# A chunked delta rule and a feed-forward layer on one Trainium2 core: the triangular inverse by 32x32 blocks and substitution in place of seven levels of doubling

## The chip, the cores and the metric

The kernel runs on one core of one Trainium2 chip, written in Python against a tile framework. The framework's scheduler sets the order of instructions on each engine, gives out the buffers of its pools and adds the semaphore waits. The engines are PE (TensorE), DVE (VectorE), ACT (ScalarE), POOL (GpSimd) and SP (which here only issues DMAs); each works through its own queue in order. The metric is the device time of one execution in microseconds (us).

## The reference

Two parts, in float32 (the inputs moe_w_in and moe_w_out arrive as float64):

```python
# q, k, v: (B=4, H=8, S=768, D=48); beta: (4, 8, 768)
k_n = k / (np.linalg.norm(k, axis=-1, keepdims=True) + 1e-06)
for t in range(S):
    y[:, :, t] = einsum('bhd,bhde->bhe', q[:, :, t], state)
    v_old = einsum('bhde,bhd->bhe', state, kt)
    state = state + bt * einsum('bhd,bhe->bhde', kt, vt - v_old)
x = y.transpose(0, 2, 1, 3).reshape(3072, 384)
h = x @ w_in                                  # w_in: 384 x 2048
out = (h * sigmoid(1.702 * h)) @ w_out        # w_out: 2048 x 384
```

The loop over time is done in chunks of 128 tokens. With T = I + strictly-lower(diag(beta) Kn Kn^T) for a chunk, it is U = T^-1 (beta V - beta Kn S), Y = Q S + strictly-lower(Q Kn^T) U, S += Kn^T U. T^-1 is a 128x128 triangular inverse for every chunk, batch and head: 6 x 4 x 8 = 192 of them.

## The kernel before

A unit is one chunk c of one batch b, all eight heads: 6 x 4 = 24 units, in the order c outer, b inner. Batches don't depend on each other; within a batch the state S_bd carries from chunk to chunk.

- load (L71) issues three DMAs on SP per unit (K, q into QP, V), two units ahead.
- prepare (L197) makes what doesn't need the state: normalised keys kn (POOL: L204 ksq, L208 rn by pow, L211; DVE: L206 sum, L209, L210), kb = beta kn (L212), beta V (L215), their transposes on PE (psT, L223: kn, kb, q, four each), the scores psG (L237, 256 columns, 48 rows of contraction) and their masked eviction LM (L241 DVE, L246 POOL).
- The rest of prepare (L252 to L294) is the inverse by doubling. X holds the inverses of T's diagonal blocks of size s; seven levels s = 1, 2, ..., 64. A level does psE = T X (L259), E = psE times a mask (L264, DVE), psXT (L280) and psX (L288), each evicted by ACT (L284, L293). Each line is four 128x128x128 matmuls for each of two halves hh of the heads.
- advance (L298) is the step of a unit: psK (L305), R = V - psK (L310), psU = XT R (L313), U (L317), psS (L322) and S_bd (L345), psY (L330, L335), x (L340, ACT), three transposes psXT (L351) into xT (L352).
- The feed-forward part of chunk c runs over the tokens of all four batches (512) and is handed out in four steps, one per unit of chunk c + 1 (L402): mm1 (L357) does four ph of three matmuls of 512 columns for each gT tile, each ph evicted by the gelu on ACT (L367); mm2 (L370) does sixteen matmuls of 384 columns for one po, copied by DVE (L378) and stored by SP (L379).
- load_weights (L176) and from_double (L134) bring the weights in 14 parts: a DMA on ACT's queue and fourteen DVE operations (L156 to L170) that make float32 of float64.

The order is that of the scheduler, which starts from the driver's order: while PE works at prepare(n + 1), advance(n) and a quarter of the feed-forward part of the chunk before are placed between. PSUM is split into ps_big (4 buffers: psT, psG, psE, psXT, psX), ps_seq (2: the step) and ps_moe (2: ph and po).

```python
    for n, (c, b) in enumerate(units):
        ...
        if n + 1 < len(units):
            prepare(n + 1)
        ...
        advance(n, xTs[c])
        if c > 0:
            feed_forward(c - 1, xTs[c - 1], b)
```

Of the kernel before, what the change touches and what calls it, by code (L numbers as in the profile page):

```python
# [9 lines left out]
I32 = mybir.dt.int32  # L10
I64 = mybir.dt.int64
# [7 lines left out]
def kernel(  # L19
# [28 lines left out]
    NTB = B * C  # L48
    FQ = 4
    assert S % C == 0 and H == 8 and D <= DP and DM == H * D == KC * 128  # L50
    assert NTB == 512 and B == 4 and FC == 4 * FQ
# [6 lines left out]
    ps_moe = ctx.enter_context(tc.tile_pool(name="ps_moe", bufs=2, space=PSUM))  # L58

    units = [(c, b) for c in range(NC) for b in range(B)]  # L60

    # rows of 64 to a head, so that a transposed head starts at partition 0 or 64
    KN = [cpool.tile([128, H, DP], F32, name=f"KN{i}") for i in range(3)]
    KB = [cpool.tile([128, H, DP], F32, name=f"KB{i}") for i in range(2)]
    QP = [cpool.tile([128, H, DP], F32, name=f"QP{i}") for i in range(3)]
    for t in KN + KB + QP:
        nc.vector.memset(t, 0.0)
# [3 lines left out]
    def load(n):  # L71
        c, b = units[n]
        K = io.tile([128, H, D], F32, tag="K", name="K", bufs=2)
        V = io.tile([128, H, D], F32, tag="V", name="V", bufs=4)
        for dst, src in ((K, k), (QP[n % len(QP)][:, :, 0:D], q), (V, v)):
            nc.sync.dma_start(
                out=dst, in_=src[b, :, c * C : (c + 1) * C, :].rearrange("h p d -> p h d")
            )
        loaded[n] = K, V

    bt = cpool.tile([NBH, S], F32, name="bt")
# [5 lines left out]
    ident = cpool.tile([128, 128], F32, name="ident")  # L87
    make_identity(nc, ident)
    upper = cpool.tile([128, 1, 128], F32, name="upper")
    nc.gpsimd.memset(upper, 1.0)  # L90
    nc.gpsimd.affine_select(
        out=upper, in_=upper, compare_op=ALU.is_ge, fill=0.0, base=-1,
        pattern=[[0, 1], [1, 128]], channel_multiplier=-1,
    )
    half = cpool.tile([128, H], F32, name="half")
    nc.gpsimd.memset(half, 0.5)

    def block_mask(name, s, transposed=False):
        """I - M: M is 1 in the lower left (upper right, transposed) quarter of each 2s block."""
        m = cpool.tile([128, 128], F32, name=name)  # L100
        nb = 128 // (2 * s)
        nc.gpsimd.memset(m, 0.0)
        part = m.rearrange("p (n j) -> p n j", j=2 * s)
        part = part[:, :, s : 2 * s] if transposed else part[:, :, 0:s]
        lo = 0 if transposed else s
        nc.gpsimd.memset(part, -1.0)
        nc.gpsimd.affine_select(
            out=part, in_=part, compare_op=ALU.is_ge, fill=0.0, base=-lo,
            pattern=[[-2 * s, nb], [0, s]], channel_multiplier=1,
        )  # L110
        nc.gpsimd.affine_select(
            out=part, in_=part, compare_op=ALU.is_ge, fill=0.0, base=lo + s - 1,
            pattern=[[2 * s, nb], [0, s]], channel_multiplier=-1,
        )
        make_identity(nc, m, nomemset=True)
        return m.rearrange("p (o j) -> p o j", o=1)

    levels = [1, 2, 4, 8, 16, 32, 64]
    emask = {s: block_mask(f"em{s}", s) for s in levels}
    emask_t = block_mask("em1t", 1, True)  # L120

    S_bd = cpool.tile([128, B, NP, 2, D], F32, name="S_bd")
    nc.vector.memset(S_bd, 0.0)
# [10 lines left out]
    def from_double(dst, src, n):  # L134
        """dst: n float32 to a partition; src: as many float64, rounded to nearest.

        DVE has no float64: the words are taken apart. The upper 23 bits of the fraction with
        the exponent moved (896 less, which in its low 8 bits flips the top one) make a float,
        the last 29 bits a second one of that scale, and their sum is rounded once. What
        float32 hasn't the exponents for becomes 0 or inf.  # L140
        """
        raw = wk.tile([128, n], I64, tag="gT", name="raw", bufs=4)
        nc.scalar.dma_start(out=raw.rearrange("p (f d) -> p f d", d=src.shape[-1]), in_=src)
        words = raw.bitcast(I32).rearrange("p (n two) -> p n two", two=2)
        lo, hi = words[:, :, 0], words[:, :, 1]
        tmp = wk.tile([128, 2, n], I32, tag="gT", name="tmp", bufs=4)
        t0, t1 = tmp[:, 0], tmp[:, 1]
        t0f, w = t0.bitcast(F32), dst.bitcast(I32)
        ts, stt, tt = (
            nc.vector.tensor_scalar, nc.vector.scalar_tensor_tensor, nc.vector.tensor_tensor,  # L150
        )
        AND, OR, XOR = ALU.bitwise_and, ALU.bitwise_or, ALU.bitwise_xor
        SHL, SHR = ALU.logical_shift_left, ALU.logical_shift_right
        SIGN, INF = -(1 << 31), 0x7F800000

        ts(w, hi, 0x0FFFFFFF, 3, op0=AND, op1=SHL)  # L156
        stt(out=w, in0=hi, scalar=SIGN, in1=w, op0=AND, op1=OR)
        stt(out=w, in0=lo, scalar=29, in1=w, op0=SHR, op1=OR)
        ts(w, w, 0x40000000, None, op0=XOR)
        ts(t0, w, SIGN | INF, None, op0=AND)  # L160
        ts(t1, lo, 0x1FFFFFFF, None, op0=AND)
        stt(out=t0f, in0=t1, scalar=2.0**-52, in1=t0f, op0=ALU.mult, op1=ALU.mult)
        tt(dst, dst, t0f, op=ALU.add)

        ts(t0, hi, 20, 0x7FF, op0=SHR, op1=AND)
        ts(t1, t0, 897.0, -1.0, op0=ALU.is_ge, op1=ALU.mult)
        stt(out=t1, in0=t0, scalar=1150.0, in1=t1, op0=ALU.is_le, op1=ALU.mult)
        stt(out=w, in0=t1, scalar=SIGN, in1=w, op0=OR, op1=AND)
        ts(t1, t0, 1150.0, float(INF), op0=ALU.is_gt, op1=ALU.mult)
        tt(w, w, t1, op=OR)  # L170

    N_IN, F_OUT = 1024, 2
    parts_in = KC * DFF // N_IN
    n_parts = parts_in + FC // F_OUT

    def load_weights(part):  # L176
        if part < parts_in:
            j, f0 = part % KC, part // KC * N_IN
            dst = w_in[:, j, f0 : f0 + N_IN]
            src = moe_w_in[j * 128 : (j + 1) * 128, f0 : f0 + N_IN].rearrange(  # L180
                "p (o f) -> p o f", o=1
            )
            n = N_IN
        else:
            f0 = (part - parts_in) * F_OUT
            dst = w_out[:, f0 : f0 + F_OUT, :].rearrange("p f d -> p (f d)")
            src = moe_w_out[f0 * 128 : (f0 + F_OUT) * 128, :].rearrange("(f p) d -> p f d", p=128)
            n = F_OUT * DM
        if src.dtype == F32:
            nc.scalar.dma_start(out=dst.rearrange("p (f d) -> p f d", d=src.shape[-1]), in_=src)  # L190
        else:
            from_double(dst, src, n)

# [1 line left out]
    ready = {}  # L195

    def prepare(n):  # L197
        c, b = units[n]
        K, V = loaded.pop(n)
        kn, kb, qp = KN[n % len(KN)], KB[n % len(KB)], QP[n % len(QP)]  # L200
# [11 lines left out]
        nc.gpsimd.tensor_tensor(  # L212
            kb[:, :, 0:D], kn[:, :, 0:D], bc.broadcast_to([128, H, D]), op=ALU.mult
        )
        nc.gpsimd.tensor_tensor(V, V, bc.broadcast_to([128, H, D]), op=ALU.mult)  # L215

        knT = wk.tile([128, NP, 128], F32, tag="knT", name="knT")
        kbqT = wk.tile([128, 2, NP, 128], F32, tag="kbqT", name="kbqT", bufs=3)
        for src, dst, on_act in ((kn, knT, 0), (kb, kbqT[:, 0], 1), (qp, kbqT[:, 1], 1)):
# [4 lines left out]
            if on_act:  # L224
                nc.scalar.activation(dst, psT, ACT.Copy)  # L225
            else:
                nc.vector.tensor_copy(dst, psT)  # L227

        # LM[hh][:, j, 0] = T^T, LM[hh][:, j, 1] = strict_upper(Kn Q^T), head 2j + hh
        LM = []  # L230
        for hh in range(2):
            lm = wk.tile([128, NP, 2, 128], F32, tag="LM", name="LM", bufs=4)
            pr = slice(hh * 64, hh * 64 + D)
            for g in range(NP // 2):
                psG = ps_big.tile([128, 2, 2, 128], F32, tag="big", name="psG")
                for i in range(2):
# [12 lines left out]
            )  # L249
            LM.append(lm)  # L250

        X, XT = [None, None], [None, None]  # L252
        for s in levels:
            last = s == levels[-1]
            E = [None, None]
# [180 lines left out]
```

## Time and profile before

| | before |
|---|---|
| median of 3 runs | 1660.29 us (1658.6 to 1660.74) |
| span of the profiled execution | 1659.9 us |
| PE busy | 1581.8 us, 95% of the span |
| DVE / ACT / POOL busy | 557.4 / 413.0 / 243.1 us |
| matmul records on PE | 10254 |
| DMA | 33.05 MB, 81526 packets, mean 20 GB/s |

The profile shows one execution. Its times are us from the span's start, and ns where a mean of one instruction is given. In a row of a timeline come start, length, engine, line, operation, the tile written and the tiles read, the shape and the count, and in square brackets how long the engine had been idle and who ended that. In a row of a group come the count, busy us and mean ns of one, then the idle time before them and its releasers. In a row of a window: the stretch, its length, busy time and count of each engine (PE, PEld, DVE, ACT, POOL), the granted PE clock (1.00 is full), the DMA share and GB/s. In the chain of waits a row is start, length and what the chain ran through; "issue" is time in which nothing that the profile shows was waited for. In an excerpt of the order stand the line, the operation, the tile written and those read, the shape of the result and a count.

### The profile page before, as it was taken

To read this page: it belongs to the slowest core of one execution; us is meant where nothing else is said; L and a number is where in the kernel's file an instruction comes from. 1 tells how busy PE (TensorE), PEld (TensorE's weight loads), DVE (VectorE), ACT (ScalarE), POOL (GpSimd) and SP (SyncE) were. 2 spreads that over 40 slices of the span, in tenths; PEclk is the share of its full clock that TensorE was granted. 3 is DMA by queue.
4 is the path that set the end of the run, shared out by engine and by line. 5 is a ranking of instruction groups with operands and counts; after the bars stand their busy time and mean duration, and the time that the engine had idled before them with its cause. 6 is when DMAs were issued, how large, how long until landed. Compare 5 with 4: busy or idle time off the path is not lost.

```text
span 1659.9 us, 23464 instructions
## 1 busy us (share of the span) xinstructions
PE 1581.8 (95%) x10254; PEld 1303.3 (79%) x10254; DVE 557.4 (34%) x866; ACT 413.0 (25%) x698; POOL 243.1 (15%) x265
## 2 busy tenths in 40 slices
PE   3887889999999999999999999999999999999999
PEld 3887789968779779688797797886978978869645
DVE  7998993322223212222222132222221321222000
ACT  0321223323213133232132331222322313323020
POOL 7224111220101101201111012011010110000000
PEclk9987989999999999999999999999999999999999
DMA  4211200000000000000000000000000000000000
GB/s 105 90 56 53 91 20 10 15 15 6 10 20 6 24 6 11 15 6 20 24 6 10 6 11 24 6 19 15 6 10 10 16 10 1 1 1 1 20 0 19
DMA packets 81526, 33.05 MB, mean 20 GB/s; under 512 B 75504, under 2 KB 78576, under 8 KB 80656
## 3 DMA queue, kind: packets, MB, share of 16 engines
q1 hardware_dynamic: 78336, 18.88, 5.3%
q10 hardware_dynamic: 3088, 12.68, 2.2%
q8 instruction: 80, 1.31, 0.3%
q14 instruction: 22, 0.18, 0.0%
HBM read 26.84 MB, written 4.72 MB: 19 GB/s over the span
## 4 chain that ended last, share of the span: by engine, by line
PE 50%; issue 33%; POOL 9%; DVE 5%; DMA 3%; POOLq 0%; ACT 0%; ACTq 0%
PE psE L259 15%; PE psXT L280 13%; PE psX L288 10%; PE po L373 6%; PE ph L363 3%; DMA K<-in_k_dram 3%; POOL rn L208 2%; POOL LM L246 2%; POOL V L215 2%; POOL KN L211 1%; PE psU L313 1%; DVE E L264 1%; POOL ksq L204 1%; PE psS L322 1%; DMA V<-in_v_dram 1%
## 5 line engine op out<-in xcount | busy, mean ns | idle before, releaser
L264 DVE TENSOR_TENSOR E<-psE,em 128x512 f32<-128x512 f32 x336 | 231.5, 691 | 493.6 <-PE psE L259 493.2
L280 PE MATMUL psXT<-XT,E 128*128 128x128 f32 x2304 | 310.2, 279 | 10.7 <-DVE E L264 10.5
L280 PEld LDWEIGHTS psXT<-XT,E 128*128 128x128 f32 x2304 | 279.2, 191 | 15.9 <-DVE E L264 14.3
L284 ACT ACTIVATE XT<-psXT 128x512 f32<-128x512 f32 x240 | 143.3, 597 | 542.0 <-PE psXT L280 542.0
L373 PE MATMUL po<-w_out,gT 128*128 128x384 f32 x768 | 254.3, 488 | 0.0
L288 PE MATMUL psX<-E,XT 128*128 128x128 f32 x1920 | 253.6, 275 | 0.0
L363 PE MATMUL ph<-xT,w_in 128*128 128x512 f32 x576 | 253.6, 594 | 0.0
L259 PE MATMUL psE<-X,LM 128*128 128x128 f32 x1920 | 246.9, 281 | 0.1
L259 PEld LDWEIGHTS psE<-X,LM 128*128 128x128 f32 x1920 | 232.6, 191 | 4.4 <-ACT X L293 0.3
L288 PEld LDWEIGHTS psX<-E,XT 128*128 128x128 f32 x1920 | 233.7, 192 | 0.0
L373 PEld LDWEIGHTS po<-w_out,gT 128*128 128x128 f32 x768 | 143.5, 190 | 93.7 <-issue 0.5
L363 PEld LDWEIGHTS ph<-xT,w_in 128*128 128x128 f32 x576 | 107.1, 190 | 123.2 <-issue 122.9
L293 ACT ACTIVATE X<-psX 128x512 f32<-128x512 f32 x240 | 143.3, 597 | 68.0 <-PE psX L288 68.0
L211 POOL TENSOR_TENSOR KN<-K,rn 128x384 f32<-128x384 f32 x24 | 23.9, 995 | 607.7 <-PE psS L322 580.3
L367 ACT ACTIVATE gT<-ph 128x512 f32<-128x512 f32 x96 | 57.3, 597 | 204.4 <-PE ph L363 204.4
L246 POOL TENSOR_SCALAR_AFFINE_SELECT LM<-LM 128x512 f32<-128x512 f32 x48 | 32.5, 677 | 452.4 <-DVE LM L241 452.4
L259 PE MATMUL psE<-ident,LM 128*128 128x128 f32 x384 | 65.0, 322 | 35.4 <-POOL LM L246 35.4
L259 PEld LDWEIGHTS psE<-ident,LM 128*128 128x128 f32 x384 | 55.3, 222 | 47.8 <-POOL LM L246 47.8
L378 DVE COPY o<-po 128x384 f32<-128x384 f32 x24 | 13.4, 558 | 236.3 <-PE po L373 236.3
L237 PE MATMUL psG<-kbqT,knT 48*128 48x256 f32 x384 | 76.5, 411 | 3.2 <-DVE knT L227 2.5
L227 DVE COPY knT<-psT 128x512 f32<-128x512 f32 x24 | 16.5, 688 | 169.5 <-PE psT L223 169.5
L225 ACT ACTIVATE kbqT<-psT 128x512 f32<-128x512 f32 x48 | 26.2, 595 | 184.3 <-PE psT L223 184.3
(88 smaller groups left out, 1136.2 us busy)
## 6 DMA issues: line engine op xcount, KB each, us to landing
raw<-in_moe_w_in_dram ACTq DMA_DIRECT2D x6, 1024.0 KB, 5.7
raw<-in_moe_w_out_dram ACTq DMA_DIRECT2D x8, 768.0 KB, 4.4
K<-in_k_dram SPq DMA_DIRECT2D x24, 192.0 KB, 2.6
V<-in_v_dram SPq DMA_DIRECT2D x24, 192.0 KB, 2.8
QP<-in_q_dram SPq DMA_DIRECT2D x24, 192.0 KB, 2.7
out_dram<-o SPq DMA_DIRECT2D x24, 192.0 KB, 1.9
bt<-in_beta_dram ACTq DMA_DIRECT2D x1, 96.0 KB, 2.8
```

Of the source, the lines that this page charges most:

```text
L211: nc.gpsimd.tensor_tensor(kn[:, :, 0:D], K, rn.broadcast_to([128, H, D]), op=ALU.mult)
L237: nc.tensor.matmul(psG[:, i], lhsT=knT[pr, 2 * g + i, :], rhs=kbqT[pr, :, 2 * g + i, :], start=True, stop=True,)
L246: nc.gpsimd.affine_select(out=lm[:, :, 0, :], in_=lm[:, :, 0, :], compare_op=ALU.not_equal, fill=1.0, base=0, pattern=[[0, NP], [-1, 128]] ...
L259: nc.tensor.matmul(psE[:, j, :], lhsT=LM[hh][:, j, 0, :], rhs=ident if s == 1 else X[hh][:, j, :], start=True, stop=True,)
L264: nc.vector.tensor_tensor(E[hh], psE, emask[s].broadcast_to([128, NP, 128]), op=ALU.mult)
L280: nc.tensor.matmul(psXT[:, j, :], lhsT=E[hh][:, j, :], rhs=XT[hh][:, j, :], start=True, stop=True,)
L284: nc.scalar.activation(newT, psXT, ACT.Copy)
L288: nc.tensor.matmul(psX[:, j, :], lhsT=XT[hh][:, j, :], rhs=E[hh][:, j, :], start=True, stop=True,)
L293: nc.scalar.activation(X[hh], psX, ACT.Copy)
L363: nc.tensor.matmul(ph, lhsT=w_in[:, j, f * 128 : (f + 1) * 128], rhs=xT[:, j, :], start=(j == 0), stop=(j == KC - 1),)
L367: nc.scalar.activation(g[:, i, :], ph, ACT.Gelu_apprx_sigmoid)
L373: nc.tensor.matmul(po, lhsT=gT[c, f // FQ][:, f % FQ, b * C : (b + 1) * C], rhs=w_out[:, f, :], start=(f == 0), stop=(f == FC - 1),)
```

## The change

- The inverse is taken apart in 32x32 diagonal blocks. prepare leaves the scores of kn with kn scaled by beta in their rows (Nn, scaled as DVE evicts psG), and those with q in M (ACT, masked by POOL afterwards). kb is gone; V gets its beta in advance, on DVE. psG's heads alternate between the two halves.
- For each unit, four DMAs write the 32x32 diagonal blocks of Nn to DRAM (Nd) and one reads them back into NT, where every partition holds one block: 4 batches x 4 blocks x 8 heads = 128.
- invert(c) works on the 128 blocks of a whole chunk at once, on DVE: 15 substitution steps (a multiply and a sum each) on both 16x16 halves, then the 16x16 corner by two sets of four products (a multiply and a sum each); between them ACT copies one half of YB into X1 (L267 of the new kernel). YB goes to DRAM in four pieces Yb.
- assemble(n) reads a unit's blocks back (four DMAs into XT, four into XO), makes the 32x32 corners of the 64x64 blocks with ps1 and ps2 (PE), the 64x64 corner with ps3 and ps4, with 32x32 transposes on DVE, and evictions on DVE (P1, P3) and ACT (l32, L335, L359).
- The driver prepares and inverts a chunk as a whole: four assemblies and steps of chunk c, then prepare and invert of chunk c + 1, then the feed-forward part of chunk c, in two halves of two batches (256 columns for ph, two ph to a PSUM tile and a gelu).
- The weights come in 28 parts, with seven DVE operations each in place of fourteen, all asked for after the first chunk's steps. The DVE products P share the buffers of gT (five in place of four).

The diff, cut to its core:

```diff
 def prepare(n):
-    nc.gpsimd.tensor_tensor(kb[:, :, 0:D], kn[:, :, 0:D], bc.broadcast_to([128, H, D]), op=ALU.mult)
-    nc.gpsimd.tensor_tensor(V, V, bc.broadcast_to([128, H, D]), op=ALU.mult)
...
-    X, XT = [None, None], [None, None]
-    for s in levels:
...
+    for g in range(0, NP, 2):
+        ps = [ps_big.tile([128, 2, 2, 128], F32, tag="big", name="psG") for _ in range(2)]
+        for i in range(2):
+            for hh in range(2):
+                pr = slice(hh * 64, hh * 64 + D)
+                nc.tensor.matmul(ps[hh][:, i], lhsT=kqT[pr, g + i, 0, :], rhs=kqT[pr, g + i, :, :], start=True, stop=True)
+        for hh in range(2):
+            nc.vector.tensor_tensor(Nn[:, hh, g : g + 2, :], ps[hh][:, :, 0, :],
+                bhg[:, hh, g : g + 2].broadcast_to([128, 2, 128]), op=ALU.mult)
+            nc.scalar.activation(M[:, hh, g : g + 2, :], ps[hh][:, :, 1, :], ACT.Copy)
...
+    for blk in range(NB):
+        r = slice(blk * BS, (blk + 1) * BS)
+        nc.sync.dma_start(out=Nd[blk * H : (blk + 1) * H].rearrange("h i k -> i h k"),
+            in_=Nn[r, :, :, r].rearrange("i hh g k -> i (hh g) k"))
+    nc.sync.dma_start(out=NT[c][b * NB * H : (b + 1) * NB * H], in_=Nd)
+
+def invert(c):
...
+    for i in range(1, HS):
+        P = wk.tile([128, 2, i, i], F32, tag="gT", name="P", bufs=5)
+        tt(P, diag(Nf, i * BS, [[0, i], [1, i]]), diag(Yf, 0, [[BS, i], [1, i]]), op=ALU.mult)
+        red(diag(Yf, i, [[BS, i]]), P, axis=AX.X, op=ALU.add, negate=True)
+    X1 = wk.tile([128, HS, HS], F32, tag="X1", name="X1", bufs=1)
+    nc.scalar.activation(X1, halves(YB)[1].rearrange("p l i -> p i l"), ACT.Copy)
+    for j in range(0, HS, Q):
+        dots(A[:, j : j + Q, :], ..., Q, HS, HS - j, False)
+    for i in range(0, HS, Q):
+        dots(YB[:, 0:HS, HS + i : HS + i + Q], ..., HS, Q, i + Q, True)
+    for b in range(B):
+        nc.sync.dma_start(out=Yb, in_=YB[b * NB * H : (b + 1) * NB * H])
+
+def assemble(n):
+    for blk in range(NB):
+        nc.sync.dma_start(out=xt[r, :, :, r]..., in_=Yb[blk * H : (blk + 1) * H]...)
+    for p, hh in quads:
+        nc.sync.dma_start(out=XO[qd * BS : (qd + 1) * BS], in_=Yb[p0 : p0 + NP]...)
+    for p, hh in quads:
+        nc.scalar.activation(l32[o, :, o], Nn[od, hh, :, ev], ACT.Copy)
+        nc.vector.transpose(xe[o, :, o], xt[ev, hh, :, ev])
+    for g in range(NP):
+        nc.tensor.matmul(ps1[:, g], lhsT=l32[:, g, :], rhs=XO[:, g, :], start=True, stop=True)
+    nc.vector.tensor_copy(P1, ps1)
+    for g in range(NP):
+        nc.tensor.matmul(ps2[:, g], lhsT=xe[:, g, :], rhs=P1[:, g, :], start=True, stop=True)
+    for p, hh in quads:
+        nc.scalar.activation(xt[ev, hh, :, od], ps2[qd * BS : (qd + 1) * BS], ACT.Copy, scale=-1.0)
+    nc.vector.transpose(xa[e, :, e], flat[e, :, e])
+    nc.vector.transpose(xa[o, :, o], flat[o, :, o])
+    nc.vector.transpose(xa[o, :, e], flat[e, :, o])
+    for h in range(H):
+        nc.tensor.matmul(ps3[:, h, :], lhsT=Nf[hi, h, lo], rhs=flat[hi, h, hi], start=True, stop=True)
+    nc.vector.tensor_copy(P3, ps3)
+    for h in range(H):
+        nc.tensor.matmul(ps4[:, h, :], lhsT=xa[:, h, :], rhs=P3[:, h, :], start=True, stop=True)
+    nc.scalar.activation(flat[lo, :, hi], ps4, ACT.Copy, scale=-1.0)

 def advance(n, xT):
+    nc.vector.tensor_tensor(V, V, psK, op=ALU.subtract)
+    nc.vector.tensor_tensor(V, V, betaT[:, c, b].broadcast_to([128, H, D]), op=ALU.mult)
...
+def feed_forward(c, b0, xT):
+    for part in range(FC // FQ):
+        for i in range(0, FQ, 2):
+            ph = ps_moe.tile([128, 2, NTH], F32, tag="moe", name="ph")
+            ...
+            nc.scalar.activation(g[:, i : i + 2, :], ph, ACT.Gelu_apprx_sigmoid)
+    for i in range(HB):
+        po = ps_moe.tile([128, DM], F32, tag="moe", name="po")
...
+prepare_chunk(0)
+for c in range(NC):
+    for b in range(B):
+        assemble(c * B + b)
+        advance(c * B + b, xTs[-1])
+    if c == 0:
+        for part in range(n_parts):
+            load_weights(part)
+    if c + 1 < NC:
+        prepare_chunk(c + 1)
+    for i in range(B // HB):
+        feed_forward(c, i * HB, xTs[i])
```

More of the change, by code (lines that the diff above doesn't have):

```diff
@@ L79, in load @@
         loaded[n] = K, V
+    for t in KN + QP:
+        nc.vector.memset(t, 0.0)
     bt = cpool.tile([NBH, S], F32, name="bt")
@@ L195 @@
     ready = {}
+    NT = {}
+    Yd = {}
     def prepare(n):
@@ L223, in prepare @@
                 nc.tensor.transpose(psT[:, j, :], flat[:, j * 128 : (j + 1) * 128], ident)
[L224 to L236, printed above, removed]
+            nc.scalar.activation(kqT[:, :, i, :], psT, ACT.Copy)
@@ L237, in prepare @@
+        Nn = wk.tile([128, 2, NP, 128], F32, tag="Nn", name="Nn", bufs=4)
+        M = wk.tile([128, 2, NP, 128], F32, tag="M", name="M", bufs=4)
+        bhg = bc.rearrange("p (g hh) -> p hh g", hh=2)
+        for g in range(0, NP, 2):
[3 more added lines that the diff above has]
+                    pr = slice(hh * 64, hh * 64 + D)
                     nc.tensor.matmul(
-                        psG[:, i], lhsT=knT[pr, 2 * g + i, :], rhs=kbqT[pr, :, 2 * g + i, :],
+                        ps[hh][:, i], lhsT=kqT[pr, g + i, 0, :], rhs=kqT[pr, g + i, :, :],
@@ L298, in advance @@
     def advance(n, xT):
         c, b = units[n]
-        kn, V, kbqT, LM, XT = ready.pop(n)
-        R = V
+        kn, V, kqT, Nn, M = ready.pop(n)
+        xt = XT[n % len(XT)]
         if c > 0:
@@ L330, in advance @@
                 nc.tensor.matmul(
-                    psY[:, 2 * j : 2 * j + 2, :], lhsT=kbqT[:, 1, j, :], rhs=S_bd[:, b, j],
+                    psY[:, 2 * j : 2 * j + 2, :], lhsT=kqT[:, j, 1, :], rhs=S_bd[:, b, j],
                     start=(j == 0), stop=True, skip_group_check=True,
@@ new lines, in feed_forward @@
+    def feed_forward(c, b0, xT):
+        gT = []
+        for part in range(FC // FQ):
+            g = wk.tile([128, FQ, NTH], F32, tag="gT", name="gT", bufs=5)
+            for i in range(0, FQ, 2):
+                ph = ps_moe.tile([128, 2, NTH], F32, tag="moe", name="ph")
+                for u in range(2):
+                    f = part * FQ + i + u
+                    for j in range(KC):
+                        nc.tensor.matmul(
+                            ph[:, u], lhsT=w_in[:, j, f * 128 : (f + 1) * 128], rhs=xT[:, j, :],
+                            start=(j == 0), stop=(j == KC - 1),
+                        )
+                nc.scalar.activation(g[:, i : i + 2, :], ph, ACT.Gelu_apprx_sigmoid)
+            gT.append(g)
+        for i in range(HB):
+            b = b0 + i
+            po = ps_moe.tile([128, DM], F32, tag="moe", name="po")
+            for f in range(FC):
@@ L363, in mm1 @@
                 nc.tensor.matmul(
-                    ph, lhsT=w_in[:, j, f * 128 : (f + 1) * 128], rhs=xT[:, j, :],
-                    start=(j == 0), stop=(j == KC - 1),
-                )
-            nc.scalar.activation(g[:, i, :], ph, ACT.Gelu_apprx_sigmoid)
-        gT[c, part] = g
-    def mm2(c, b):
-        po = ps_moe.tile([128, DM], F32, tag="moe", name="po")
-        for f in range(FC):
-            nc.tensor.matmul(
-                po, lhsT=gT[c, f // FQ][:, f % FQ, b * C : (b + 1) * C], rhs=w_out[:, f, :],
-                start=(f == 0), stop=(f == FC - 1),
-            )
-        o = wk.tile([128, DM], F32, tag="o", name="o")
-        nc.vector.tensor_copy(o, po)
-        nc.sync.dma_start(out=out[b * S + c * C : b * S + (c + 1) * C, :], in_=o)
@@ L404, with prepare_chunk @@
-    for step in range(4):
-        feed_forward(NC - 1, xTs[NC - 1], step)
+                    po, lhsT=gT[f // FQ][:, f % FQ, i * C : (i + 1) * C], rhs=w_out[:, f, :],
+                    start=(f == 0), stop=(f == FC - 1),
+                )
+            o = wk.tile([128, DM], F32, tag="o", name="o")
+            nc.vector.tensor_copy(o, po)
+            nc.sync.dma_start(out=out[b * S + c * C : b * S + (c + 1) * C, :], in_=o)
+    def prepare_chunk(c):
+        for b in range(B):
+            n = c * B + b
+            prepare(n)
+            if n + 2 < len(units):
+                load(n + 2)
+        invert(c)
```

319 lines of the change are left out of this document (153 added, 166 removed).

## Prediction

> **What bounds the kernel now.** I read the page first (busy shares, chain by engine), then the chain of waits in order of time, then the timeline of one unit, then the groups by form. From the page and the chain:
>
> ```profile
> PE 1581.8 (95%) x10254; PEld 1303.3 (79%) x10254; DVE 557.4 (34%) x866; ACT 413.0 (25%) x698; POOL 243.1 (15%) x265
> PE 50%; issue 33%; POOL 9%; DVE 5%; DMA 3%; POOLq 0%; ACT 0%; ACTq 0%
> 1030.03 3.10 PE psE L259 x24
> 1096.01 3.10 PE psE L259 x24
> 1574.06 41.20 PE ph L363 x96
> 1615.25 41.30 PE po L373 x128
> ```
>
> TensorE is busy for 95% of the 1659.9 us. In the chain the same piece comes back after 65.98 us: that is one unit, and there are 24. The feed-forward part of the last chunk, alone on PE, is 41.2 + 41.3 = 82.5 us. In a unit's timeline the doubling stands in one stretch, from its second psE to its last psXT:
>
> ```profile
> 1031.02 2.10 PE L259 MATMUL psE<-E,LM 128*128 128x128 f32 x16
> ...
> 1060.50 2.10 PE L280 MATMUL psXT<-XT,E 128*128 128x128 f32 x16
> ```
>
> Those six levels last from 1031.02 to about 1062.4, 31.4 us; the first level adds 2. So 33 of a unit's 66 us are the inverse, and PE hardly pauses in it: the amount of matmuls is the bound.
>
> **What goes.** 24 x 33 = 800 us. If nothing came back, 860 us would be left. What comes back decides.
>
> **What comes in, on PE.** Prices of small matmuls, from the chain near the end (start, us, what):
>
> ```profile
> 1547.64 0.86 PE psK L305 x8
> ...
> 1549.82 1.72 PE psU L313 x16
> 1551.54 0.93 PE psY L330 x8
> ...
> 1553.15 1.72 PE psY L335 x16
> ...
> 1555.58 0.41 PE psXT L351 x3
> ```
>
> Two records make a float32 matmul, and a record costs 0.11 us at 48 and at 96 columns alike. The assembly of a unit has four ps1 and four ps2 of 32 columns (0.87 us per four) and eight ps3 and eight ps4 of 64 x 64, which no row shows: I take psY's 1.72 for each eight, the nearest row. The Trainium skill ("TensorE: Matmul & The Clock Gate", LDWEIGHTS) says that loading weights takes time by their columns; 64 columns would halve ps3 and ps4, and the total would be some 41 us lower. No row here has such a load, so I stay with the row.
>
> On PE the assembly of unit n+1 is now woven into the step of unit n (ps1 to ps4: assembly; psU, psS, psY, psXT2: the step):
>
> ```order
> L356 MATMUL ps4_2695<-P3_2693,XA0_87 64x64 x8
> L325 MATMUL ps1_2768<-XO_2751,L320_85 128x32 x4
> L377 MATMUL psU_2712<-V_1314,XT0_82 128x48 x8
> L330 MATMUL ps2_2775<-P1_2773,XE0_86 128x32 x4
> L386 MATMUL psS_2723<-U_2721,KN4_79 128x96 x4
> L394 MATMUL psY_2728<-S_bd_125,kqT_2090 128x96 x4
> L399 MATMUL psY_2728<-U_2721,M_2104 128x48 x8
> L349 MATMUL ps3_2787<-XT1_83,Nn_2159 64x64 x5
> L415 MATMUL psXT2_2745<-ident_108,x_2741 128x128 x3
> ```
>
> Before, a feed-forward matmul stood behind psU at this place:
>
> ```order
> L313 MATMUL psU_2865<-R_2863,XF_2447 128x48
> L363 MATMUL ph_2904<-xT_883,w_in_186 128x512
> L322 MATMUL psS_2876<-U_2874,KN2_75 128x96 x4
> L330 MATMUL psY_2881<-S_bd_175,kbqT_2155 128x96 x4
> L335 MATMUL psY_2881<-U_2874,LM_2174 128x48
> ```
>
> So the cover of the evictions changes: it was the feed-forward part, now it is the neighbour's assembly. The hops and evictions, in the timeline and the groups:
>
> ```profile
> 1062.44 0.54 PE L313 MATMUL psU<-R,XF 128*128 128x48 f32 x4
> 1062.82 1.52 PE L373 MATMUL po<-w_out,gT 128*128 128x384 f32 x4
> 1063.02 0.56 DVE L317 COPY U<-psU 128x384 f32<-128x384 f32 x1 [1.63 <-PE psU L313]
> 1067.89 0.49 ACT L340 ACTIVATE x<-psY 128x384 f32<-128x384 f32 x1 [4.65 <-PE psY L335]
> 1068.43 0.55 PE L351 MATMUL psXT<-ident,x 128*128 128x128 f32 x3
> L284 ACT ACTIVATE XT<-psXT 128x512 f32<-128x512 f32 x240 | 143.3, 597 | 542.0 <-PE psXT L280 542.0
> L264 DVE TENSOR_TENSOR E<-psE,em 128x512 f32<-128x512 f32 x336 | 231.5, 691 | 493.6 <-PE psE L259 493.2
> ```
>
> From PE's next matmul (1062.82) to the eviction 0.2 us; from x's end (1068.38) back to PE 0.05. ACT takes 0.49 at 384 and 0.60 at 512 elements, so 0.28 at 128; DVE 0.56 and 0.69, so 0.30. A woven unit: psU 1.72 + ps2 0.87 + psS 0.87 + psY 0.93 + 1.72 + ps3 1.72 + psXT 0.41 + psK 0.86 + ps4 1.72 + ps1 0.87 = 11.7 us, and 0.4 of waits (for x and P3): 12.1. The first unit of a chunk has no neighbour: its ps1 to ps4 (5.2) wait 0.55 for P1, 1.35 for four L335 copies, 0.94 for P3: 8.0. The last one's step alone is 6.9. **Stage A** (four assemblies and steps) = 8.0 + 3 x 12.1 + 6.9 = 51 us. DVE's seven 32x32 transposes a unit have no row; at a copy's 0.30 (128 elements) and 0.43 (256) DVE has under 6 us a unit beside PE's 12, so they are free; at four times that they would not be.
>
> **Stage B** (four prepares). With 256 columns a record:
>
> ```profile
> 1023.81 2.96 PE L237 MATMUL psG<-kbqT,knT 48*128 48x256 f32 x16
> ```
>
> 4 x 2.96 + 32 transposes at 0.11 (kb's sixteen are gone, with its POOL multiply, off the path) + 1.3 of waits for kqT = 17 us. The heads now alternate, which may overlap them; at the floor of 0.11 a record it would be 7 us. The 12 ph matmuls woven into A and B cost 5 us (24 of 192 half-width records, 41.2 in all). A 256-wide ph record is half a 512-wide one, 0.215, above the 0.11 floor: the halved feed-forward part costs nothing by itself.
>
> **The wait that comes in.** ACT behind a chunk's last evictions, before (gT is the gelu):
>
> ```order
> L284 ACTIVATE XF_4056<-psXT_4057 128x512
> L340 ACTIVATE x_4100<-psY_4087 128x384
> L367 ACTIVATE gT_4109<-ph_4110 128x512
> L367 ACTIVATE gT_4109<-ph_4115 128x512
> L367 ACTIVATE gT_4109<-ph_4120 128x512
> ```
>
> and now (M is the last eviction of prepare, X1 the copy inside the next chunk's inverse):
>
> ```order
> L214 ACTIVATE M_3147<-psG_3159 128x256
> L267 ACTIVATE X1_3225<-YB_88 128x256
> L432 ACTIVATE gT_3260<-ph_3261 128x512
> L432 ACTIVATE gT_3260<-ph_3269 128x512
> L432 ACTIVATE gT_3277<-ph_3278 128x512
> ```
>
> X1 waits for all 15 substitution steps of the next chunk, and the 16 gelus of this chunk stand behind it. ps_moe has two buffers, and the woven ph have filled both; PE's next ph waits. How long, from:
>
> ```profile
> L170 DVE TENSOR_TENSOR w_in<-w_in,tmp 128x1024 int32<-128x1024 int32 x6 | 7.3, 1218 | 0.0
> L206 DVE TENSOR_REDUCE ssq<-ksq 128x8 f32<-128x384 f32 x24 | 13.2, 551 | 2.1 <-POOL ksq L204 1.2
> 1071.96 0.17 DVE L209 TENSOR_SCALAR rn<-rn 128x8 f32<-128x8 f32 x1 [1.76 <-POOL rn L208]
> 1072.17 0.20 DVE L210 RECIPROCAL rn<-rn 128x8 f32<-128x8 f32 x1
> 1066.15 0.37 SPq L76 DMA_DIRECT2D K<-in_k_dram  x1
> K<-in_k_dram SPq DMA_DIRECT2D x24, 192.0 KB, 2.6
> out_dram<-o SPq DMA_DIRECT2D x24, 192.0 KB, 1.9
> ```
>
> The last Nn 0.6 (hop, 256 elements); four issues at 0.37 ahead of the last Nd 1.5; its landing 2.2 (between 1.9 and 2.6); NT's landing 2.1; 30 dependent DVE operations on 2 x 2480 elements, 1.04 ns each + 0.155 + 0.04 an operation = 11.0; X1 0.4; the first gelu 0.6; hops 0.2: **18.6 us** a chunk with PE idle. The rest of the inverse (16 operations on 10,240 elements, 14 us), Yd's round trip and the XT loads lie beside the feed-forward part, 77 us long, and cost nothing; without it some 20. Behind a stall the clock (last three columns: granted clock, DMA share, GB/s):
>
> ```profile
> 128.00:134.00 6.00, 4.96 (x44) 4.83 (x44) 6.00 (x8) 2.29 (x4) 0.00 (x0) 1.00 0.20 45
> 140.00:146.00 6.00, 6.00 (x27) 5.34 (x25) 6.00 (x10) 0.00 (x0) 6.00 (x1) 0.50 0.00 1
> 158.00:164.00 6.00, 6.00 (x50) 6.00 (x49) 5.39 (x11) 2.00 (x4) 0.00 (x0) 0.90 0.00 0
> 135.44 5.62 PE L237 MATMUL psG<-kbqT,knT 48*128 48x256 f32 x16 [2.49 <-DVE knT L227]
> ```
>
> It falls from 1.00 to 0.50 over idle gaps of a few us (psG takes 5.62 there instead of 2.96) and comes back after some 5 us of work: I charge 3 us. **A chunk**: 51 + 17 + 5 + 18.6 + (82.5 - 5.2) + 3 = 172 us (before 264), four times 688.
>
> **The start and the end.**
>
> ```profile
> L204 POOL TENSOR_TENSOR ksq<-K 128x384 f32<-128x384 f32 x24 | 20.1, 838 | 39.5 <-DMA K<-in_k_dram 39.5
> L208 POOL TENSOR_TENSOR rn<-ssq,half 128x8 f32<-128x8 f32 x24 | 42.3, 1763 | 58.5 <-DVE ssq L206 58.5
> L211 POOL TENSOR_TENSOR KN<-K,rn 128x384 f32<-128x384 f32 x24 | 23.9, 995 | 607.7 <-PE psS L322 580.3 <-PE psT L223 16.3 <-DVE rn L210 11.1
> L162 DVE SCALAR_TENSOR_TENSOR tmp<-tmp 128x1024 f32<-128x1024 int32 x6 | 7.3, 1217 | 0.0
> L162 DVE SCALAR_TENSOR_TENSOR tmp<-tmp 128x768 f32<-128x768 int32 x8 | 7.7, 958 | 0.1
> L159 DVE TENSOR_SCALAR w_in<-w_in 128x1024 int32<-128x1024 int32 x6 | 4.2, 697 | 0.0
> L159 DVE TENSOR_SCALAR w_out<-w_out 128x768 int32<-128x768 int32 x8 | 4.4, 556 | 0.0
> 1656.57 0.56 DVE L378 COPY o<-po 128x384 f32<-128x384 f32 x1 [9.76 <-PE po L373]
> ```
>
> POOL has 0.84 + 1.76 + 1.0 = 3.6 us a unit. On SP the first Nd stands behind a K load that waits for the fifth KN: I put that at 27 us and the last NT's landing at 43 (35 to 55), the inverse 25 behind it: 68. Then DVE: conversions 12 x (4 x 0.415 + 3 x 0.70) + 16 x (4 x 0.345 + 3 x 0.57) = 95, the first assemblies 21, the next prepares 11, gaps 10 (0 to 30): 205. The next inverse's steps stand behind all that on DVE, and X1 behind them: 217. The first feed-forward part ends at 217 + 77 + 2 = 296. The last chunk: 51 - 3.5 (no psS) + 82.5 + 1 = 131; from the last o to the span's end 3.4 us, as before.
>
> **Sum**: 296 + 688 + 131 + 3 = 1118 us. The span of the profiled execution, 1659.9, is 0.4 under the median of the runs, so nothing is corrected.
>
> **Rivals.** (1) *The gelu isn't held*, X1 being done before ph needs its buffer. Then 4 x 21.6 goes, and 29 at the start (po waits for the conversions to 205 instead): 1003 us. For it: only that the stall is read from two queues and no row; against: X1 needs the fourth unit's psG and four landings behind it. 8%. (2) *Slow clock all through A and B*: some 62 us of matmuls a chunk at half speed give 1118 + 4 x 62 + 45 = 1411; for half of the time 1265. For it: the 0.50 rows, after a gap of 2.49; against: PE pauses in A for 9% of the time, in pieces under 1.4 us. The Trainium skill ("TensorE: Matmul & The Clock Gate", Part 1) puts the fall after an idle window of about 3.4 us; by that rule only the gelu stall trips it and 1118 stands, and the 2.49 gap speaks for less than that. 12%. (3) *Slower than before*: the small transfers stand one behind another on SP. A unit has 14 (Nd, NT, Yb, XT, XO); all exposed at 2.6 they are 36 us, 24 times 874: some 1960. It decides from 23 us a unit, 9 of the 14; I count two a chunk. The Trainium skill ("DMA: Bandwidth & Descriptors", Specifications) says that pieces under 512 B are read, modified and written; these are 128 B, and K's of 192 B (48 floats a head) land in 2.6. 3%.
>
> **How the numbers follow.** The forecast has 77%. Its own unknowns: down 12 (ps3 and ps4 overlapped as psG is), 50 (psG at the floor), 20 (stall and start at their low ends), so 1035; up 72 (3 us more waiting a unit in A), 25 (start), so 1215, which takes in a part of rival 2. A change under 0.2%, 3 us, couldn't be told from none: 1%. Faster 96%, slower 3%.
>
> **What would show it.** Right: ACT idle for about 18 us a chunk before X1, PE as long before ph; the same piece coming back after 172 us; the clock at 1.00 in A. Wrong: ph running on behind psG, A taking 80, or PE waiting elsewhere for a landing of NT, XO or XT.

## The result and the profile after

| | before | after |
|---|---|---|
| median of the runs | 1660.51 us (1658.6 to 1662.05, 4 runs) | 1283.05 us (1276.61 to 1286.69, 4 runs) |
| ratio | | 0.772, 95% interval 0.770 to 0.774 |
| the profiled execution, span | 1659.9 us | 1281.6 us |
| mean granted clock | 0.98 | 0.77 |

The change is faster, by 377 us; 542 had been forecast (1118), and 1283 lies above the range of 1035 to 1215.

The page of after, with busy time, PE's and the clock's 40 slices, and the chain by engine:

```profile
PE 1024.0 (80%) x4974; PEld 837.8 (65%) x4974; DVE 438.9 (34%) x1020; ACT 203.5 (16%) x488; POOL 117.0 (9%) x112
PE   2408971199999299999389999479999669999998
PEclk9855665599758689857789857779956879955799
PE 31%; DVE 3%; DMA 1%; ACT 0%; SPq 0%; issue 0%; ACTq 0%
```

PE was busy for 95% before and is for 80% now, in a span 23% shorter, and the clock, which had been near 1.00, drops to about half in every chunk, also in slices where PE shows 9. Two losses are to be told apart. Both stand in the stretches of one chunk and of the end (columns: stretch, length, busy of PE, PEld, DVE, ACT and POOL, granted clock, DMA share, GB/s):

```profile
922.10:984.00 61.90, 59.81 (x316) 56.34 (x315) 18.23 (x45) 10.71 (x33) 4.05 (x4) 0.53 0.07 15
984.00:1013.60 29.60, 28.58 (x235) 24.18 (x233) 11.43 (x26) 11.34 (x29) 3.34 (x4) 1.00 0.19 36
1013.60:1038.00 24.40, 0.03 (x2) 0.00 (x0) 17.14 (x42) 2.38 (x7) 1.09 (x1) 0.59 0.07 16
1042.00:1117.60 75.60, 75.60 (x288) 54.58 (x287) 5.12 (x11) 8.36 (x14) 0.00 (x0) 1.00 0.10 22
1121.00:1199.00 78.00, 77.21 (x392) 72.65 (x393) 18.48 (x41) 10.84 (x30) 0.00 (x0) 0.50 0.02 4
```

The first row is most of stage A (assemblies and steps): PE is busy for 59.8 of 61.9 us, and the clock stands at 0.53. The second holds the rest of A, B and 16 of the 24 woven ph records at 1.00; the first eight of them, from 968.8 on, stand in the first row. The third is the pause, without PE work. The fourth is the feed-forward part. The last chunk's stage A (fifth row) runs at 0.50 throughout.

In the chain of the same chunk (start, length, what) the step's matmuls show what that costs:

```profile
922.29 0.82 PE ps L325 x8
923.48 1.09 PE ps L330 x8
...
931.60 3.44 PE psU L377 x16
...
952.18 3.44 PE psU L377 x16
...
974.68 3.28 PE psU L377 x16
...
991.38 1.86 PE psU L377 x16
```

psU takes 3.44 us where the prediction had 1.72, and a woven unit takes 20.6 us (931.60 to 952.18) where it had 12.1. Sixteen records come at 1.86 again once the clock is back, in the fourth unit. The pause, in the waits of PE and in ACT's timeline:

```profile
PE ph L428 <- ACT gT L432: 142.6, 5, 45.4
PE ps L325 <- DMA XO<-Yb: 42.1, 1, 42.1
```

```profile
1031.38 0.65 ACT L267 ACTIVATE X<-YB 128x256 f32<-128x256 f32 x1 [16.55 <-DVE YB L263]
1037.36 1.08 ACT L432 ACTIVATE gT<-ph 128x512 f32<-128x512 f32 x2 [5.33 <-DVE A L243]
```

PE waits 142.6 us for a gelu, five times, once 45.4. The gelu stands behind X1, as forecast, but after X1 it waits another 5.33 us for a reduction of the inverse (A, L243), with whose result it has nothing to do.

### The profile page after: what moved, and what is told of

It is laid out like the page before. It is cut to its first block, busy times and chain, and to the rows that moved or that the text cites. A ratio compares the mean times of both kernels' runs of the same rounds, so it can differ in the third digit from the quotient of the medians.

```text
span 1281.6 us, 12617 instructions
## 1 busy us (share of the span) xinstructions
PE 1024.0 (80%) x4974; PEld 837.8 (65%) x4974; DVE 438.9 (34%) x1020; ACT 203.5 (16%) x488; POOL 117.0 (9%) x112
## 5 line engine op out<-in xcount | busy, mean ns | idle before, releaser
L428 PE MATMUL ph<-xT,w_in 128*128 128x256 f32 x1152 | 284.6, 406 | 142.6 <-ACT gT L432 142.6
L428 PEld LDWEIGHTS ph<-xT,w_in 128*128 128x128 f32 x1152 | 230.9, 205 | 178.5 <-ACT gT L432 144.9
L377 PEld LDWEIGHTS psU<-V,XT 128*128 128x128 f32 x384 | 77.2, 304 | 1.6
L377 PE MATMUL psU<-V,XT 128*128 128x48 f32 x384 | 78.0, 383 | 0.0
L205 PE MATMUL psG<-kqT 48*128 48x256 f32 x384 | 62.9, 458 | 10.2 <-ACT kqT L194 8.0
L399 PE MATMUL psY<-U,M 128*128 128x48 f32 x384 | 68.9, 352 | 0.0
L399 PEld LDWEIGHTS psY<-U,M 128*128 128x128 f32 x384 | 68.3, 274 | 0.2
L205 PEld LDWEIGHTS psG<-kqT 48*128 48x128 f32 x384 | 42.9, 221 | 23.1 <-ACT kqT L194 13.3
L349 PE MATMUL ps<-XT,Nn 64*64 64x64 f32 x384 | 45.1, 293 | 5.6 <-ACT XT L335 5.6
L356 PE MATMUL ps<-P,XA 64*64 64x64 f32 x384 | 43.6, 295 | 5.4 <-DVE P L353 5.4
L193 PE MATMUL psT<-ident,KN 128*128 128x128 f32 x96 | 18.5, 325 | 35.9 <-POOL KN L186 23.1
```

What stands on the lines that cost most here:

```text
L205: nc.tensor.matmul(ps[hh][:, i], lhsT=kqT[pr, g + i, 0, :], rhs=kqT[pr, g + i, :, :], start=True, stop=True,)
L349: nc.tensor.matmul(ps3[:, h, :], lhsT=Nf[hi, h, lo], rhs=flat[hi, h, hi], start=True, stop=True)
L356: nc.tensor.matmul(ps4[:, h, :], lhsT=xa[:, h, :], rhs=P3[:, h, :], start=True, stop=True)
L377: nc.tensor.matmul(psU[:, h, :], lhsT=xt[:, h % 2, h // 2, :], rhs=V[:, h, :], start=True, stop=True)
L399: nc.tensor.matmul(psY[:, h, :], lhsT=M[:, h % 2, h // 2, :], rhs=U[:, h, :], start=(c == 0 and h == 0), stop=True, skip_group_check=True,)
L428: nc.tensor.matmul(ph[:, u], lhsT=w_in[:, j, f * 128 : (f + 1) * 128], rhs=xT[:, j, :], start=(j == 0), stop=(j == KC - 1),)
```

## The experiments

Ten kernels. Nine are timed against the kernel before on their chip, and the times are medians; the one with TensorE alone ran once.

**What the gelu waits for.** The inverse's products P and the gelu's output gT share one tag with five buffers. Three kernels take the candidates apart.

X1 on DVE:

```diff
-        nc.scalar.activation(X1, halves(YB)[1].rearrange("p l i -> p i l"), ACT.Copy)
+        nc.vector.tensor_copy(X1, halves(YB)[1].rearrange("p l i -> p i l"))
```

> X1 is copied by DVE instead of ACT, nothing else. Theory A (the gelus are held by X1 ahead of them on ACT, as the prediction had it): with X1 off that queue the feed-forward part runs on behind psG, TensorE's pauses of some 25 us a chunk go, five of them: 1283 - 115 to 125 = about 1160. Theory B (the first gelu is held longer by its buffer: gT and the inverse's products P share one tag with five buffers, and the trace has the gelu wait 25.3 us in five for a reduction of the inverse that ends up to 5.3 us after X1): the pause stays as long as it is, 1283 within 5.

Measured 1284.66 (ratio to before 0.773, interval 0.772 to 0.775): no change, theory B's number. PE's wait for the gelu is still there:

```profile
PE ph L428 <- ACT gT L432: 144.0, 5, 45.6
```

P with a buffer of its own:

```diff
-            P = wk.tile([...], F32, tag="gT", name="P", bufs=5)
+            P = wk.tile([...], F32, tag="P", name="P", bufs=1)
```

> P gets a tag and one buffer of its own, X1 stays on ACT. Theory A and B alike: the gelus now wait for X1 alone, which saves the 25.3 us that the trace shows behind X1 in five chunks: about 1258. If neither queue nor buffer holds them, nothing changes.

Measured 1143.9 (0.690, 0.685 to 0.695): 139 us faster, over five times what either theory gave it. The row of ph in the groups of this kernel (busy, mean ns, idle before):

```profile
L428 PE MATMUL ph<-xT,w_in 128*128 128x256 f32 x1152 | 279.2, 399 | 0.0
```

Its idle time is 0.0, with X1 still on ACT. ACT's order in one chunk says why:

```
after:                                   P with its own buffer:
L214 ACTIVATE M_3147<-psG_3159           L214 ACTIVATE M_2216<-psG_2228
L267 ACTIVATE X1_3225<-YB_88             L432 ACTIVATE gT_2346<-ph_2347
L432 ACTIVATE gT_3260<-ph_3261           ... (five more gelus)
L432 ACTIVATE gT_3260<-ph_3269           L267 ACTIVATE X1_2294<-YB_88
```

The scheduler had put the gelus behind X1 because a gT could have no buffer before the P's of the inverse were through. Without the shared buffer it puts six of them in front. X1's place on ACT was a symptom.

Both edits:

> Both edits: X1 on DVE and P with a buffer of its own. Theory B: only now is nothing of the inverse ahead of the gelus, TensorE's idle time before ph of 142.6 us goes but for the first chunk's wait for the weights (some 20 of its 45): about 1160, and the clock no longer falls between psG and ph. Theory A: the same as X1 alone.

Measured 1141.01 (0.689, 0.685 to 0.694): as P's buffer alone. The shared buffer is the whole pause; X1 is nothing.

**What holds the clock down in stage A.** Wide matmuls in the lead-in of a chunk, where PE waits for evictions:

```diff
+        if b == 0 and c > 0:
+            wide = ps_moe.tile([128, 512], F32, tag="moe", name="wide")
+            for i in range(3):
+                nc.tensor.matmul(wide, lhsT=P1..., rhs=w_in[:, 0, 0:512], start=True, stop=True)
```

and two each behind ps3 (from xt) and ps4 (from P3).

> Seven float32 matmuls of 512 columns with a result that nobody reads are added in the first unit of each chunk but the first: three behind ps2, two behind ps3, two behind ps4, where TensorE waits for evictions in the lead-in; 7 x 0.86 = 6 us of work a chunk, five chunks, some 15 of the 30 us in time that is idle now. Theory 1 (what the small matmuls do sets the clock, not the waits): the clock falls to 0.50 within one or two windows of 3.4 us behind the last wide one and stays there for the next two units as now: 1285 to 1305. Theory 2 (the waits of the lead-in drop the clock, and it then needs more than small matmuls to rise, but not to stay): the clock stays at 1.00 through the whole of stage A, which saves about half of the 58 us at 0.50 in four chunks and of the last chunk's 78: 1283 - 4 x 25 - 33 + 15 = about 1165.

Measured 1270.55 (0.764, 0.760 to 0.767), 12 us faster than after with some 30 us of matmuls more. Neither theory had that number. The windows of one chunk say how it comes about:

```profile
920.00:933.00 13.00, 13.00 (x90) 8.94 (x88) 3.52 (x9) 2.37 (x8) 1.03 (x2) 1.00 0.10 16
933.10:936.50 3.40, 3.19 (x30) 2.94 (x29) 1.95 (x8) 1.56 (x5) 1.33 (x1) 1.00 0.40 74
936.50:974.00 37.50, 37.50 (x193) 35.12 (x191) 11.36 (x26) 5.04 (x15) 0.83 (x1) 0.50 0.03 6
974.00:1005.00 31.00, 29.18 (x240) 24.75 (x239) 12.19 (x28) 12.03 (x30) 4.10 (x4) 1.00 0.19 35
```

The lead-in now runs at 1.00. Then comes a stretch of psY, ps2, psXT2 and the first records of psK and ps3, in which PE pauses for 0.2 of 3.4 us, and behind it the clock falls and stays at 0.50 through 37.5 us without a pause. So it falls late, as theory 1 has it: not for waiting. But what is bridged does hold, which theory 1 had not counted.

TensorE alone, with no wait at all:

```diff
+    for n in [512, 128, 96, 64, 48, 32, 48, 64, 96, 128, 256, 512, 48, 512]:
+        ps = ps_moe.tile([128, 512], F32, tag="moe", name=f"w{n}_")
+        for i in range(count):
+            nc.tensor.matmul(ps[:, 0:n], lhsT=wt[:, i % 8, :], rhs=mv[:, 0:n], start=True, stop=True)
```

> Nothing of the kernel is computed: the output is zeros. TensorE alone, float32 matmuls back to back with eight different weights of 128x128 loaded in turn, with no wait in them: 27 us at full clock each of 512, 128, 96, 64, 48, 32, 48, 64, 96, 128, 256, 512, 48 and 512 columns. Theory 1 (a window of 3.4 us counts by how much of it columns are streamed; in the traces the clock fell behind windows with under 0.38 to 0.41 of a full clock's columns and rose behind windows with over 0.8 of a half clock's): 128 columns hold 1.00; 96 (0.73 of the time at 0.11 us a record) hold it; 64 (0.48) is near the limit; 48 (0.36) and 32 (0.24) fall to 0.50 within two windows although TensorE never waits; on the way up 48 and 64 stay at 0.50, 96 is near the limit, 128 brings 1.00 back. A record of 48 columns takes 0.11 us at 1.00 and 0.22 at 0.50. Theory 2 (only time in which TensorE waits lowers the clock): 1.00 throughout behind the first stretch.

The chain, one row a stretch (512, 128, 96, 64, 48, 32 columns, then 48, 64, 96 and 128 again, and, after one of 256, a later stretch of 512):

```profile
18.87 28.50 PE w__100 L77 x62
47.38 27.24 PE w__133 L77 x244
74.62 27.22 PE w__257 L77 x244
101.84 27.22 PE w__381 L77 x244
129.06 46.63 PE w__505 L77 x244
175.69 52.03 PE w__629 L77 x244
227.72 52.08 PE w__753 L77 x244
279.80 52.08 PE w__877 L77 x244
331.88 29.41 PE w__1001 L77 x244
361.29 27.27 PE w__1125 L77 x244
...
415.33 26.61 PE w__1313 L77 x62
```

Two stretches of it with the same 64 columns, on the way down and on the way up:

```profile
104.00:128.00 24.00, 24.00 (x217) 24.00 (x217) 0.00 (x0) 0.00 (x0) 1.00 0.01 1
282.00:325.00 43.00, 43.00 (x203) 43.00 (x203) 0.00 (x0) 0.00 (x0) 0.50 0.00 0
```

PE is busy for the whole of both. On the way down 128, 96 and 64 columns hold 1.00 (27.2 us for 244 records, 0.11 each); at 48 the clock falls; on the way up 48 and 64 stay at 0.50 (52.1 us), and 96 brings 1.00 back. In columns: 62 records of 512 take 26.6 us at full clock (the last row), 1193 columns a us. At 0.11 us a record, 64 columns are then 48% of what could stream, 48 are 36%; at 0.50, 64 are 50% and 96 some 75% of what the half clock could stream. **A full clock stays at 48% and falls at 36%; a half clock stays at 50% and rises at 75%.** Theory 2 is out.

The kernels fit, by estimates from the counts and shapes of their rows: the woven unit from 931.60 to 952.18 streams 6784 columns, 330 a us, 55% of the half clock's, which lies between the 50% that left it down and the 75% that brought it up; the 3.4 us ahead of 936.50 above stream some 37% of a full clock's. Only the columns were varied, in one execution; whether weights on 64 rows, as those of ps3 and ps4, count like those on 128 was not tried.

The rule of the Trainium skill ("TensorE: Matmul & The Clock Gate", Part 1) that the clock falls after an idle window of about 3.4 us agrees in the length of the window (in these traces the clock changes at multiples of 3.413 us: its stretch at 0.50 in the last chunk of the kernel after is 78.51 us, 23 of them) and not in what counts as idle: PE was never idle here, and for 0.2 us in the 3.4 ahead of 936.50 above.

**The order of the program.** The second half of a chunk's feed-forward part is issued behind the next chunk's stage A:

```diff
+        if c > 0:
+            feed_forward(c - 1, HB, xT_held)
+        xT_held = xTs[1]
         if c + 1 < NC:
             prepare_chunk(c + 1)
-        for i in range(B // HB):
-            feed_forward(c, i * HB, xTs[i])
+        feed_forward(c, 0, xTs[0])
+        if c + 1 == NC:
+            feed_forward(c, HB, xT_held)
```

> Only the order of the program: the second half of a chunk's feed-forward part is issued behind the next chunk's stage A instead of ahead of it, with a third xT buffer; X1 and P as they are. TensorE then has wide matmuls between the small ones from the start of stage A. Theory 1 (what the matmuls do sets the clock): stage A stays at 1.00, its 58 us at 0.50 in each of four chunks cost about 25 less and the last chunk's 78 about 33 less; the pause of 25 us before ph stays: 1283 - 133 = about 1150. Rival (what holds the clock down in stage A is the chain of short waits behind each eviction, or the woven matmuls delay that chain as much as the clock gives): stage A grows by the 41 us it takes in, without a gain: 1270 to 1300.

Measured 1176.77 (0.707, 0.705 to 0.710): 106 us faster, 27 short of the sum. The windows of one chunk, stage A first, the pause third:

```profile
655.00:720.00 65.00, 64.52 (x441) 58.81 (x440) 23.47 (x59) 13.59 (x38) 10.12 (x10) 0.77 0.15 29
720.00:772.00 52.00, 51.36 (x260) 37.78 (x259) 8.39 (x22) 13.08 (x31) 6.31 (x6) 1.00 0.17 35
772.70:796.40 23.70, 0.89 (x9) 0.72 (x7) 17.79 (x43) 1.84 (x5) 1.09 (x1) 0.62 0.13 25
```

Stage A is at 0.77 instead of 0.53, and the pause is as long as it was.

The same order with P in its own buffer (and X1 on DVE, o and P1 with one buffer each):

> The same order, with P in a buffer of its own and X1 on DVE (o and P1 with one buffer each, for the space). If the shared buffer and the slow clock in stage A are two separate losses, their gains add up: 1141 less what the slow clock still costs there, 102 windows of 3.4 us at 0.50 = 348 us, half of them lost = 174, of which some 25 a chunk can come back: 985 to 1030. If one stands in for the other (the feed-forward part had covered the inverse, and half of it now lies in stage A): TensorE waits for XO instead, 20 us a chunk: 1080 to 1110.

Measured 996.1 (0.600, 0.598 to 0.602). One chunk, and the clock's slices of the page:

```profile
555.00:590.00 35.00, 34.32 (x305) 31.28 (x303) 18.04 (x46) 11.44 (x32) 6.50 (x6) 1.00 0.19 35
590.00:632.00 42.00, 41.73 (x242) 31.55 (x242) 8.46 (x21) 4.55 (x11) 6.58 (x6) 1.00 0.11 24
632.00:648.00 16.00, 15.36 (x110) 11.74 (x108) 5.29 (x14) 9.48 (x26) 3.27 (x3) 1.00 0.46 92
648.00:695.90 47.90, 47.90 (x195) 36.27 (x196) 28.28 (x59) 6.86 (x14) 1.09 (x1) 1.00 0.19 42
```

```profile
PEclk9999999999999999977999999999999999999999
```

A chunk takes 141 us, PE busy for 139 of it at 1.00. The two losses are separate, and the gains more than add up: 139 for the buffer and 106 for the order are 245, together they give 287. This version is the best of all that ran.

Some 30 of the 42 between 245 and 287 lie in stage A. With the order alone it falls as in the row above in three chunks (1 to 3), with both edits in one, the two sevens; 65 us at 0.77 lose some 15, an estimate from that row. Why the clock stays up in the other chunks was not looked into.

The first seven nines of that line are not a measurement. The trace's first record of the clock is at 185 us, and ahead of it the profile shows 1.00 whatever the clock is. The same sixteen records of psU show that it was at half:

```profile
140.24 3.63 PE L377 MATMUL psU<-V,XT 128*128 128x48 f32 x16
191.48 1.99 PE L377 MATMUL psU<-V,XT 128*128 128x48 f32 x16
```

**Two parts of the change alone, on the kernel before.** Each feed-forward matmul of 512 columns as two of 256:

> The kernel before, with each feed-forward matmul of 512 columns as two of 256, nothing else: the step of the prediction that priced the halves at nothing. By it, 1660 within 5. Rival (each record costs its weight load, or a fixed time, on top): 1152 more records at 0.1 us = 1660 + 115 = 1775.

Measured 1660.02 (0.999, 0.998 to 1.000): free, as priced. The new conversion of the weights:

> The kernel before with the new conversion of the weights, nothing else: 97 us of DVE in place of 176 in the first 260. TensorE pauses there for some 34 us between 40 and 280 and loses a few more by the clock. If DVE's share of that is what holds it: 1660 - 25 to 40. If the loads or the chain of each unit's evictions hold it: 1660 within 5.

Measured 1630.68 (0.980, 0.978 to 0.983): 31 us faster. From 40 to 280 us PE's idle time falls from 34.3 to 14.9. So a part of the 377 us belongs to the conversion and not to the inverse: 31 us on the kernel before. What it is worth in the new order no run shows.

**The start of the best version.** The conversions there stand between the first inverse's steps on DVE. Here P of chunk 0 shares the conversion's buffers again, and eight parts are converted ahead of the inverse:

```diff
-            P = wk.tile([...], F32, tag="P", name="P", bufs=1)
+            P = wk.tile([...], F32, tag="P" if c else "gT", name="P", bufs=1 if c else 5)
...
+            if c == 0:
+                load_weights(2 * b)
+                load_weights(2 * b + 1)
```

> The kernel of the held order, and the start: there TensorE is busy for 45 of the first 150 us, with 58.5 us of waiting for the first XO, since DVE has a conversion between every two steps of the first inverse. Here the first chunk's products P use the conversion's buffers again, so that the conversions of w_out and the last of w_in stand behind that inverse, and eight parts of w_in are converted between the first four prepares. If the first inverse is what the start waits for, XO lands some 30 to 50 us earlier; the first stage A then has fewer wide matmuls beside it and runs at 0.50 for 50 us, which gives some 15 to 25 back: 955 to 985. If the conversions are what the start waits for (97 us of DVE, of which some 30 now lie in front), 990 to 1000.

Measured 1004.15 (0.606, 0.602 to 0.609), 8 us slower than the best version. PE's wait for the first XO falls from 58.5 to 44.5 us, and the fourth unit's psU starts at 169.84 instead of 191.48. By the second chunk the lead is gone: its first psU starts at 271.2 instead of 270.1. Between the two lies about the same work; in the rows the best version comes first, then this one, each from its trace's first record of the clock on:

```profile
185.00:270.10 85.10, 83.97 (x482) 66.29 (x481) 49.57 (x115) 25.12 (x56) 13.41 (x12) 1.00 0.23 47
163.50:271.20 107.70, 91.27 (x464) 70.03 (x464) 76.65 (x184) 25.48 (x55) 15.37 (x12) 0.86 0.31 74
```

It takes 22.6 us longer, of which 15.3 are pauses of PE (16.4 against 1.1 us) and 7.3 longer matmuls, at 0.86 instead of 1.00. DVE is busy for 76.7 us of it instead of 49.6; conversions, which now stand behind the first inverse, are some 39 of these and 6 in the best version. The longest pause, 9.0 us, is for a KN of the second chunk's prepares; what held that KN was not followed, nor the 9 us that are lost later.

## Why the prediction was wrong, point by point

The sum had 296 for the start, 4 x 172 and 131 + 3 for the end. The trace has 333, 4 x 196.3 and 164: 37 + 97 + 30 = 164 us more, which is the miss.

- **The step that failed: "the clock at 1.00 in A", with 3 us a chunk charged for it.** A and B take 91.5 us (922.1 to 1013.6) where 51 + 17 + 5 = 73 were summed, 18.5 more in each chunk, and nearly all of the 30 at the end. The prediction looked for pauses ("PE pauses in A for 9% of the time, in pieces under 1.4 us") and concluded that the clock would stay. The widths show that matmuls of 48 columns cost the clock without any pause, and that 64 columns don't bring it back. A row that the prediction shows had the sign: from 140 to 146 us PE was busy for all 6 us and the clock stayed at 0.50. Its rival 2 "for half of the time" named the effect, at 62 us a chunk for the full case, and for the wrong reason, a gap. The sentence from the Trainium skill that spoke for 1118 was an idle window's; the trace doesn't agree with it here.
- **Terms that made up for a part of it.** The clock's own price is higher than 18.5: 61.9 us at 0.53 are 33 us of work at 1.00, so some 29 a chunk, an estimate from that row. Some 9 of it were made up by terms that had been put too high, ps3, ps4 and psG (last point but one). So rival 2's 31 a chunk for the half was about the right size. That its total of 1265 comes near 1283 is in part luck: the pause and the start add some 60 us to it, and the terms put too high take some 40 back.
- **The pause of 18.6 us.** X1 ends 18.4 us behind the last psG (1013.6 to 1032.0), where the prediction's terms up to it are 17.8: nearly as forecast. The gelu comes 5.3 later: 24.4 in all. The cause given, "X1 ... and the 16 gelus of this chunk stand behind it", is a queue that was read rightly and explained wrongly. Rival 1, "the gelu isn't held", is what one changed tag brings about; it was priced at 115 less and gives 139.
- **The start.** 37 late: X1 of the second inverse comes at 246.3 instead of 217, and the gelu 5 later still. About half of the 29 is the first inverse, which ends at 82 where 68 was put: the last NT is issued at 56.7, and the steps start at 59.1 instead of 43. The other half lies between there and the second inverse's first step at 234.4, 152 us where 137 were summed. The conversion's own work was right: its groups add up to 97 us, against 95; but DVE is idle for 38.5 of the 152, where 10 were put for gaps.
- **ps3, ps4 and psG.** ps3 and ps4, put at 1.72, take 1.07 at full clock (from 922.02 to the next line's first record at 923.09, in the kernel with the wide lead-in), over a third less and not half. The rule in the Trainium skill ("TensorE: Matmul & The Clock Gate", LDWEIGHTS), by columns, points the right way; by it the row would be 0.86, an estimate. psG's sixteen records take 2.00 us in the kernel after (1003.05) where 2.96 were summed, so the alternating heads do overlap. The range's lower end had counted 50 for this, by setting psG's floor of 7 us against the 17 of the whole stage B; against psG's own 11.8 it is 4.8 a chunk, 24 in five.
- **What held.** Doubling gone, about 33 us a unit; halves of 256 free (96 ph in 20.72 us, and the run on the kernel before); the rest of the inverse and the small DMAs hidden: ps waits for XO once, in the first chunk. Rival 3 has no row for it. At 1.00 and without the pause the prediction's chunk is 172 - 18.6 - 3 = 150; the best version, which also fills the lead-in, takes 141.

## What to carry to other kernels

When work is moved off a matmul-bound engine, ask what is left beside the small matmuls: back to back, they can halve their own clock, and wide ones woven in from another stage, even at the price of a third buffer, keep it up: here half of the feed-forward part did, while seven in the lead-in held it for 13 us only. When an instruction stands behind a stranger in a queue, look first at what buffers the two share; here the scheduler ordered by what could have a buffer, so the queue showed the effect and not the cause.

## What the runs showed of the hardware

In these runs the granted clock follows how many columns stream in a window of 3.41 us and has a memory: the same 244 records of 64 columns with weights of 128 took 27.2 us when the clock came from 1.00 and 52.1 when it came from 0.50, with PE busy for 100% of both. PE's busy share in a profile says nothing of this; the row to read is the granted clock, and that only from the trace's first clock record on: in the best version it reads 1.00 ahead of 185 us, where sixteen records of psU take 3.63 us instead of 1.99. At 0.50 a record that is bound by its weight load doubles too (0.11 to 0.21 us).
